# One chunk of a weights' product from split operands, and another sequence of pieces, in a fused attention, gating and spatial-product kernel

## The chip, the cores and the metric

The kernel runs on one core of a Trainium2 chip. The metric is the device time of one launch in microseconds, taken as the median of several runs; one more execution was taken by the hardware profiler, and all rows and durations below come from it.

## The reference, cut to what matters

Three layers run one after the other on a batch of 2 sequences of 768 positions with 512 channels (8 heads of 64). All is float32.

```python
# 1: attention; scores of near keys (within 16) and of the maxima of 32-key blocks
x = softmax(concat(mask(q @ k.T), q @ k_max.T + log 32)) @ concat(v, v_mean)
# 2: causal convolution of 5 taps as a gate
gate = sigmoid(conv5(x, conv_w))
x = (gate * (x @ w_val)) @ w_out
# 3: spatial gating
h = relu(x @ w_in)                 # 512 -> 1024
u, v = h[..., :512], h[..., 512:]
v_s = w_spatial @ normalize(v) + b_spatial
out = (u * v_s) @ w_out2
```

Between layers 2 and 3 nothing stands but two products, so the kernel multiplies the weights first, `w_out @ w_in` (512 x 512 by 512 x 1024), and applies one matrix to the gated values. This **weights' product** is where the change acts.

## The kernel before, in words

**Pieces and threads.** The work is written as some forty threads (generators) that each yield after a piece: `lk`, `lq`, `lv` load one pair of heads of k, q, v; `kw` lays out a pair's keys; `score`, `at` and `pv` are scores with softmax, transposition, and attention times values with the convolution; `gate`, `val0`/`val1`, `u0`/`u1`, `v0`/`v1`, `ws`, `f0`/`f1`, `s0`/`s1`, `out2` and `r` are the later stages for the two batches; `hot` is a warm-up matmul that nobody reads; `vsum` loads and sums the rows of v by blocks (two loads of 512 KB a piece), `put` sets these means into the values.

**What sets the order.** `ORDER` (line 45) is a list of thread names; each token runs the named thread by one piece (lines 1275 to 1295), and a piece that needs others runs those first (`need`, line 1285). Every operation is only recorded then, and the position in that list is its priority. A planner (lines 214 to 420) afterwards simulates the engines with its own costs and gives each engine, at each moment, the operation that can start first, and among several that can start (within `LOOK`, line 43, 100 ns on GpSimd, 200 on SyncE, 0 on the others) the one of the earliest priority. It also hands out the 33 SBUF units and the 8 PSUM banks; banks are given strictly in the order of the recorded list. All loads go through SyncE's queue in the planner's order. All engine calls leave through line 230, so every row of the profile has L230, and tiles come by the names of their homes (`at_u` an SBUF unit, `at_ps` a PSUM bank); rows are told apart by form.

**Weights.** Weights come as raw 64-bit words (`load64`, line 553): 512 KB for 128 rows of 512, turned into float32 by a ScalarE pass into PSUM and two VectorE passes. A weight that is used "split" is stored as two parts, `hi` (a cast to float32r on ScalarE) and `lo` (the rest, a subtraction on GpSimd), and a product of split operands is three float32r matmuls, hi·hi, hi·lo and lo·hi (`mm3`, line 515), in place of one float32 matmul.

**The weights' product** (`w_product`, line 1198, thread `wp`) has two halves: n = 1 for the V half (columns 512 to 1023 of w_in), then n = 0 for the U half. Each half is four output blocks `e` of 128 x 512, and each block sums four chunks `i` of 128 rows, so there are eight chunks of four matmuls. The V half runs over chunks outside and blocks inside, with four PSUM banks open at once (line 1219), one piece a chunk; the U half runs over blocks outside (line 1205, `OUTER` = 1), one piece a block. `WHOLE` (line 38) says for each half how many of its chunks use the float32 operands whole; before, all four of both. The pieces of w_in are loaded by `in1` (V half) and `in0` (U half), those of w_out (transposed) by `wout`; whether a piece is split at load is decided in `split64`:

```python
whole = i < WHOLE[max(c, name == "ot")] and name in ("ot", "in")   # line 574
```

For w_out (`name == "ot"`) this asks the V half's number. Where the U half wants a piece of w_out split that the V half wants whole, the thread `os` (`split_late`, line 1193) splits it later; before, that thread has no pieces (line 1254).

The results are split again into hi and lo (`wv` for V, `wu` for U, line 1179) and used by `v0`, `v1`, `u0`, `u1`.

Of the kernel before, what the change touches and what calls it, by code (L numbers as in the profile page):

```python
# [34 lines left out]
OUTER, PSUMT = 1, 1  # L35


WHOLE = {0: 4, 1: 4}


SEVEN = {'val': (), 'u': (), 'v': ()}
# [1 line left out]
LOOK = {"PE": 0, "ACT": 0, "DVE": 0, "POOL": 100, "SP": 200}  # L43

ORDER = """
    in1 mask*2 hot wout hot*2 wout hot lk kw in1 lk lq wp hot*2 wout kw in1*2 lq hot score*2 wout vsum wp in0 lk in0
    wval lk wp lq in0 lq at vsum lv*2 wp lk kw score put cw lq in0 wp at kw score wu score wval lq score lk lv put*2
    score pv wp score wp at wp wval lv pv lk pv lq at wval at put pv gate val0*2 at lv lk val0 at pv val0 kw at
    score*2 pv vsum*2 wu kw wu*2 wv pv*2 gate u0*4 lq put at val0 at wv lv kw val0 score*3 kw score*3 wv*2 v0*2 val0
    at val0 at pv put pv at lv put v0 at*2 v0 at u0 pv*4 f0 lv put pv gate pv ws v0 u0 v0 u0 val1 ws gate val1 u0  # L50
    val1 s0 val1*3 ws v1 val1 out2 v1 val1 s0 f0 u1*2 f0 v1*2 f1 v1 u1 ws v1 u1 s0 out2 s0 u1 s1 u1 f0 ws f1 f0 s0
    u1 ws f1 u1 s0 s1 out2 s0 out2 ws s0*3 f0*2 s0*2 s1 f1 s1 r s1 r s1 s0 f1 s0 f1 r s1 r*2 f1 s1*2 r s1*3 r s1 r*2
    s1 r*3
"""

WIN = 10240 / 3
# [393 lines left out]
def tile_kernel(ctx, tc, q, k, v, vn, w_val, conv_w, w_out, w_in, w_sp, b_sp, w_out2, mask_l, mask_r, eye, out):  # L450
# [120 lines left out]
    def split64(name, src, c):  # L571
        third = Parts(512)
        for i in range(KT):
            whole = i < WHOLE[max(c, name == "ot")] and name in ("ot", "in")
            t = load64(src[i * P : (i + 1) * P, 1024 * c : 1024 * (c + 1)], to=wide.get() if whole else None)
# [603 lines left out]
    def halves(x):  # L1179
        hi, lo = third.get(), third.get()  # L1180
        copy("phi", hi, x)
        sub("plo", lo, x, f(hi))
        return hi, lo
# [9 lines left out]
    def split_late(i):  # L1193
        need("wout", i + 1)
        if i >= WHOLE[0]:
            W["ot", i, 0] = halves(T["ot", i, 0])

    def w_product():
# [5 lines left out]
        for n in (1, 0):  # L1204
            if n < OUTER:
                for e in range(KT):
                    po = psum()
                    for i in range(KT):
                        need("wout", i + 1)
                        need(f"in{n}", i + 1)  # L1210
                        if i < WHOLE[n]:
                            pe.matmul(po, T["ot", i, 0][:, e * P : (e + 1) * P], T["in", i, n], start=i == 0, stop=i == KT - 1)
# [7 lines left out]
            for i in range(KT):  # L1220
                need("wout", i + 1)
                need(f"in{n}", i + 1)
                if i < WHOLE[n]:
                    for e in range(KT):
# [60 lines left out]
    def need(name, n):  # L1285
        plan.needs.setdefault(plan.piece[-1], set()).add((name, n))
        while count[name] < n:
            step(name)
# [86 lines left out]
```

## Time and profile before

| | us |
|---|---|
| median of 3 runs | 262.67 |
| lowest, highest | 261.48, 264.2 |
| the profiled execution | 262.76 |
| its span, first to last instruction | 261.0 |
| TensorE busy in it | 254.6 |
| VectorE, ScalarE, GpSimd busy | 188.8, 158.9, 161.0 |

In the rows PE is TensorE, PEld its weight loads, DVE VectorE, ACT ScalarE, POOL GpSimd, SP SyncE (SPq: its queue, which issues the loads). Times are microseconds from the span's start unless marked ns. Matmuls are pipelined and their ends are modelled, so a stretch of matmuls is best read from its start to the next row's start. The float32 matmul of this kernel stands as two instructions, one from float32r operands as one; both print as f32.

### The profile page before, as it was taken

How to read it: one execution, taken by the hardware profiler on the slowest of the kernel's cores; microseconds unless marked ns; L12 is line 12 of the kernel's file. 1: busy time of each engine (PE TensorE's matmuls, PEld its weight loads, DVE VectorE, ACT ScalarE, POOL GpSimd, SP SyncE). 2: the span in 40 equal slices, each digit the busy share in tenths (PEclk: the TensorE clock that was granted, in tenths of full speed). 3: DMA queues.
4: the chain of work that ended last, by engine and by line, in shares of the span. 5: the costliest groups of instructions: out<-in, count | busy, mean ns of one | idle time of the engine just before them, and what ended most of it. 6: DMA issues, size and time to landing. Idle time of an engine off the chain costs nothing.

```text
span 261.0 us, 5401 instructions
## 1 busy us (share of the span) xinstructions
PE 254.6 (98%) x1878; PEld 217.7 (83%) x1878; DVE 188.8 (72%) x558; ACT 158.9 (61%) x440; POOL 161.0 (62%) x189
## 2 busy tenths in 40 slices
PE   7899999999999999999999999999999999999995
PEld 5355665588999989899999999899999989889884
DVE  1789979599999995779996785879777915545110
ACT  2578989999897999859352254152385534233122
POOL 6233508998977649933907449346289998885110
PEclk9999999999999999999999999999999999999999
DMA  6999999899140006740000010003022003021213
GB/s 216 400 411 407 404 222 353 268 346 291 45 124 0 4 9 180 236 133 0 4 1 0 0 52 31 0 0 83 1 82 83 0 0 121 3 80 40 80 43 121
DMA packets 10651, 31.80 MB, mean 122 GB/s; under 512 B 1520, under 2 KB 1984, under 8 KB 10624
## 3 DMA queue, kind: packets, MB, share of 16 engines
q1 hardware_dynamic: 10592, 31.43, 35.7%
q8 instruction: 15, 0.25, 0.4%
q14 instruction: 12, 0.10, 0.1%
q0 software_dynamic: 32, 0.02, 0.0%
HBM read 28.20 MB, written 3.15 MB: 120 GB/s over the span
## 4 chain that ended last, share of the span: by engine, by line
PE 75%; DMA 11%; ACT 6%; DVE 5%; issue 2%; POOL 1%; SPq 0%; POOLq 0%; DVEq 0%; ACTq 0%
PE at_ps L230 75%; DMA at_u<-in_k_dram 6%; ACT at_u L230 5%; DMA at_u<-in_vn_dram 4%; DVE at_u L230 4%; POOL at_u L230 1%; SPq L230 0%; ACT at_ps L230 0%; DVE km L230 0%; ACT xl L230 0%; POOLq L230 0%; DVE nm L230 0%; DVEq L230 0%; ACTq L230 0%
## 5 line engine op out<-in xcount | busy, mean ns | idle before, releaser
L230 PE MATMUL at_ps<-at_u,at_u 128*128 128x384 f32 (+4 forms) x1744 | 229.1, 319 | 0.7 <-POOL at_u L230 0.4
L230 PEld LDWEIGHTS at_ps<-at_u,at_u 128*128 128x128 f32 (+2 forms) x1744 | 198.8, 186 | 27.2 <-issue 9.9
L230 POOL TENSOR_TENSOR at_u<-at_u,at_u 128x384 fp32r<-128x384 f32 (+2 forms) x83 | 101.2, 1245 | 44.2 <-ACT at_u L230 43.8
L230 ACT CAST at_u<-at_u 128x384 fp32r<-128x384 f32 (+2 forms) x83 | 45.8, 589 | 44.1 <-DVE at_u L230 31.6
L230 ACT COPY at_u<-at_ps 120x384 f32<-120x384 f32 (+3 forms) x61 | 28.6, 508 | 31.5 <-PE at_ps L230 31.5
L230 DVE TENSOR_TENSOR at_u<-at_ps,at_u 128x384 f32<-128x384 f32 (+1 forms) x36 | 19.8, 552 | 32.5 <-PE at_ps L230 25.7
L230 POOL TENSOR_TENSOR at_u<-at_u,sm 128x360 f32<-128x360 f32 x32 | 25.9, 836 | 20.8 <-DVE sm L230 17.2
L230 ACT ACTIVATE at_u<-at_u,nm 128x120 f32<-128x120 f32 x96 | 36.6, 386 | 1.8 <-DVE nm L230 1.8
L230 DVE SCALAR_TENSOR_TENSOR at_u<-at_ps,cw,at_u 128x384 f32<-128x384 f32 (+3 forms) x64 | 36.5, 605 | 0.2
L230 DVE CUSTOM_DVE_ANT_0 at_u<-at_ps,mask 128x120 f32<-128x120 f32 x96 | 21.8, 273 | 1.0 <-PE at_ps L230 1.0
L230 ACT ACTIVATE at_ps<-at_u 128x512 f32<-128x512 f32 x20 | 13.1, 654 | 9.9 <-DMA at_u<-in_moe_w_out_dram 5.9
L230 ACT ACTIVATION_READ_ACCUMULATOR at_u<-at_u,nm 128x1 f32 x96 | 18.4, 191 | 0.0
L230 POOL COPY at_u<-at_u 128x320 f32<-128x320 f32 (+2 forms) x24 | 17.4, 730 | 1.2
L230 DVE TENSOR_SCALAR at_u<-at_u 128x512 uint32<-128x512 uint32 (+1 forms) x21 | 12.7, 607 | 6.7 <-DMA at_u<-in_moe_w_in_dram 5.3
L230 DVE TENSOR_TENSOR at_u<-at_u,at_u 128x256 f32<-128x256 f32 (+2 forms) x25 | 15.7, 633 | 1.4 <-DMA at_u<-in_vn_dram 1.3
L230 POOL TENSOR_TENSOR va<-va,power 128x1 f32<-128x1 f32 x12 | 7.6, 638 | 14.6 <-DVE va L230 14.6
L230 DVE SCALAR_TENSOR_TENSOR at_u<-at_u,at_u 128x384 f32<-128x384 f32 x16 | 16.2, 1019 | 0.3
L230 ACT ACTIVATE at_u<-at_ps 128x512 f32<-128x512 f32 x20 | 11.6, 598 | 7.2 <-PE at_ps L230 7.2
L230 DVE TENSOR_TENSOR at_u<-at_u 128x384 f32<-128x384 f32 (+5 forms) x31 | 14.8, 477 | 0.1
L230 DVE SCALAR_TENSOR_TENSOR at_u<-at_ps,at_u 128x512 uint32<-128x512 uint32 x20 | 13.6, 686 | 1.4 <-ACT at_ps L230 0.5
L230 PEld LDWEIGHTS at_ps<-moves,at_u 128*120 128x120 f32 x96 | 10.9, 137 | 3.7 <-issue 1.6
L230 PE MATMUL at_ps<-moves,at_u 128*120 128x128 f32 x96 | 13.6, 276 | 0.1
(38 smaller groups left out, 136.5 us busy)
## 6 DMA issues: line engine op xcount, KB each, us to landing
at_u<-in_moe_w_in_dram SPq DMA_DIRECT2D x8, 512.0 KB
at_u<-in_moe_w_out_dram SPq DMA_DIRECT2D x8, 512.0 KB, 9.6
at_u<-in_k_dram SPq DMA_DIRECT2D x8, 384.0 KB, 7.2
at_u<-in_q_dram SPq DMA_DIRECT2D x8, 384.0 KB, 6.2
at_u<-in_vn_dram SPq DMA_DIRECT2D x6, 512.0 KB
at_u<-in_v_dram SPq DMA_DIRECT2D x8, 384.0 KB, 7.3
out_dram<-at_u SPq DMA_DIRECT2D x11, 256.0 KB, 2.0
at_u<-in_moe_w_spatial_dram SPq DMA_DIRECT2D x6, 384.0 KB, 4.1
```

The lines of the kernel that those rows point to most:

```text
L230: getattr(real, method)(*[home(x) for x in args], **{k: home(x) for k, x in kw.items()})
```

## The change

`WHOLE[0]` goes from 4 to 3: the fourth chunk (i = 3) of the U half's four blocks is computed from split operands by `mm3`, in place of float32 ones. With that, w_in's fourth piece of the U half is split at load (`split64`), and the thread `os` gets four pieces, of which the fourth splits w_out's fourth piece (the first three only state their need). `ORDER` is replaced by another sequence, which has the `os` pieces in it. The planner, its costs and every other piece are the same.

```diff
-WHOLE = {0: 4, 1: 4}
+WHOLE = {0: 3, 1: 4}
...
 ORDER = """
-    in1 mask*2 hot wout hot*2 wout hot lk kw in1 lk lq wp hot*2 wout kw in1*2 lq hot score*2 wout vsum wp in0 lk in0
-    wval lk wp lq in0 lq at vsum lv*2 wp lk kw score put cw lq in0 wp at kw score wu score wval lq score lk lv put*2
-    score pv wp score wp at wp wval lv pv lk pv lq at wval at put pv gate val0*2 at lv lk val0 at pv val0 kw at
-    score*2 pv vsum*2 wu kw wu*2 wv pv*2 gate u0*4 lq put at val0 at wv lv kw val0 score*3 kw score*3 wv*2 v0*2 val0
-    at val0 at pv put pv at lv put v0 at*2 v0 at u0 pv*4 f0 lv put pv gate pv ws v0 u0 v0 u0 val1 ws gate val1 u0
-    val1 s0 val1*3 ws v1 val1 out2 v1 val1 s0 f0 u1*2 f0 v1*2 f1 v1 u1 ws v1 u1 s0 out2 s0 u1 s1 u1 f0 ws f1 f0 s0
-    u1 ws f1 u1 s0 s1 out2 s0 out2 ws s0*3 f0*2 s0*2 s1 f1 s1 r s1 r s1 s0 f1 s0 f1 r s1 r*2 f1 s1*2 r s1*3 r s1 r*2
-    s1 r*3
+    mask hot mask wout in1 wout lk in1 kw lk lq in1 wout hot*2 lq kw hot*2 in1 hot wp score*2 wp vsum wp wout in0 lk
+    kw lk in0 lq kw wval at lq in0 vsum os score*2 lv lq lv lk*2 os put cw pv put score wp hot os*2 in0 wp at wval
+    wp score lv score wp at pv lk wu lv put at score pv wp at put pv gate at wval kw wval val0 at val0*2 pv kw pv
+    val0 wu at lv score*2 vsum pv at wu kw pv gate vsum put lv wu u0*3 at lk wv u0 val0*2 lv lq score put wv kw
+    score lv lq score wv score lq score wv score val0*2 v0*2 at pv*2 at v0 at put at v0 at*2 u0 pv*4 put pv*2 u0 ws
+    u0 ws v0 f0 gate u0 gate val1*3 v0 val1 f0 val1*3 u1 s0*2 val1 ws v1 u1 f0 v1 f0 out2 u1 f0 v1 f1 u1 s0 u1 v1*3
+    u1 out2 ws*2 s0 f1 u1 out2 s0*5 s1 out2 u1 s1 s0 f1 r f0 s1 f1 ws r s1*3 ws s0 s1 f1 s0 f0 s0 s1*2 s0 r s1 r*4
+    f1 s1*2 r f1 s1*2 r*4
 """
```

## Rows read from the trace of the kernel before

**Rows 1.** The page: span, and busy time of each engine

```profile
span 261.0 us, 5401 instructions
...
PE 254.6 (98%) x1878; PEld 217.7 (83%) x1878; DVE 188.8 (72%) x558; ACT 158.9 (61%) x440; POOL 161.0 (62%) x189
```

**Rows 2.** The chain of waits, last pieces: start, duration, what

```profile
62.51 195.46 PE at_ps L230 x1411
...
257.99 0.37 ACT at_u L230
```

**Rows 3.** Table of stretches: busy time of each engine

```profile
core 0: us, PE busy (x) PEld busy (x) DVE busy (x) ACT busy (x) POOL busy (x), PEclk, DMA share, GB/s
...
8.00:20.00 12.00, 11.55 (x67) 6.19 (x68) 9.15 (x30) 7.93 (x21) 4.74 (x11) 1.00 1.02 405
20.00:31.00 11.00, 11.00 (x61) 5.80 (x62) 10.66 (x37) 10.32 (x30) 4.41 (x12) 1.00 1.03 404
...
40.00:50.00 10.00, 9.79 (x51) 4.72 (x49) 9.06 (x42) 9.91 (x43) 8.86 (x10) 1.00 0.86 304
50.00:60.00 10.00, 9.72 (x123) 7.63 (x125) 7.90 (x15) 9.96 (x26) 9.63 (x10) 1.00 1.02 342
...
80.00:100.00 20.00, 20.00 (x230) 18.56 (x229) 18.57 (x101) 18.41 (x76) 13.72 (x20) 1.00 0.05 11
```

**Rows 4.** TensorE in order of time, 8 to 28 us

```profile
8.25 3.67 PE L230 MATMUL at_ps<-at_u 128*128 128x512 f32 x8 [0.74 <-DVE at_u L230]
...
12.54 1.08 PE L230 MATMUL at_ps<-at_u,at_u 64*64 64x120 f32 x12 [0.17 <-POOL at_u L230]
...
14.70 1.07 PE L230 MATMUL at_ps<-at_u,at_u 64*64 64x120 f32 x12
...
18.48 1.09 PE L230 MATMUL at_ps<-at_u,at_u 64*64 64x120 f32 x24
19.50 3.70 PE L230 MATMUL at_ps<-at_u 128*128 128x512 f32 x8
23.04 1.88 PE L230 MATMUL at_ps<-at_u,at_u 128*128 128x512 f32 x4
24.75 0.82 PE L230 MATMUL at_ps<-moves,at_u 128*120 128x128 f32 x6
25.41 2.74 PE L230 MATMUL at_ps<-at_u,at_u 128*128 128x512 f32 x6
```

**Rows 5.** TensorE in order of time, around 105 us

```profile
104.61 3.01 PE L230 MATMUL at_ps<-at_u,at_u 128*128 128x512 f32 x12
107.46 1.47 PE L230 MATMUL at_ps<-moves,at_u 128*120 128x128 f32 x12
```

**Rows 6.** Groups of instructions by form: count, busy us, mean ns, idle before

```profile
L230 POOL TENSOR_TENSOR at_u<-at_u,at_u 128x512 fp32r<-128x512 f32 x16 | 21.4, 1347 | 7.3 <-ACT at_u L230 7.0
...
L230 DVE SCALAR_TENSOR_TENSOR at_u<-at_ps,at_u 128x512 uint32<-128x512 uint32 x20 | 13.6, 686 | 1.4 <-ACT at_ps L230 0.5 <-PE at_ps L230 0.2
...
L230 ACT ACTIVATE at_ps<-at_u 128x512 f32<-128x512 f32 x20 | 13.1, 654 | 9.9 <-DMA at_u<-in_moe_w_out_dram 5.9 <-DMA at_u<-in_moe_w_in_dram 4.0
...
L230 ACT CAST at_u<-at_u 128x512 fp32r<-128x512 f32 x16 | 9.6, 625 | 1.1 <-DVE at_u L230 1.1
```

**Rows 7.** SyncE's queue in order of time; the page's loads of w_out

```profile
8.98 0.33 SPq L230 DMA_DIRECT2D at_u<-in_moe_w_out_dram  x1
10.36 1.43 SPq L230 DMA_DIRECT2D at_u<-in_vn_dram  x2
...
36.65 0.33 SPq L230 DMA_DIRECT2D at_u<-in_moe_w_in_dram  x1
...
at_u<-in_moe_w_out_dram SPq DMA_DIRECT2D x8, 512.0 KB, 9.6
```

## The prediction

> **What bounds the kernel now.** I read the page first: TensorE is busy 254.6 of the 261.0 us span; VectorE, the next, 188.8 us [rows 1]. The chain of waits says the same from the other end: its last link but one is an unbroken run of 195.46 us of matmuls that begins at 62.51 us [rows 2]. From there on, nothing but the sum of TensorE's work sets the end, and a changed sequence can gain nothing, only open a gap. So the second view is the table of stretches, to see where TensorE is not full [rows 3]: between 8 and 20 us it idles 0.45 us, between 40 and 50 us 0.21, between 50 and 60 us 0.28, together 0.94 us; 20 to 31 us and 80 to 100 us are full. Before 8.25 us it runs only warm-up matmuls. The granted clock is 1.00 in each of these stretches, so the higher of the two levels (2.4 GHz). The same table shows what feeds it: between 8 and 31 us the loads run at 404 to 405 GB/s with the DMA engines 100% occupied. Up to about 40 us the order of loads decides which pieces TensorE can take; between 40 and 60 us ScalarE (9.91 and 9.96 of 10 us) and GpSimd (8.86 and 9.63) are nearly full as well. The early 60 us are the place where this change acts, in both of its parts.
>
> **The split chunk on TensorE.** The weights' product has eight chunks of four matmuls with 512 columns. A float32 one stands in the trace as two instructions: a chunk is the row of x8 at 19.50 us, which runs until the next row begins at 23.04, so 3.54 us, 0.443 us an instruction [rows 4]. From split operands a chunk takes 4 x 3 = 12 matmuls, each one instruction. The nearest row is a product of twelve such instructions with 512 columns at 104.61 us, with the next row at 107.46: 2.85 us, 0.238 each [rows 5]. The chunk costs 3.54 - 2.85 = 0.69 us less. Lower bound of the gain nothing (if TensorE stands waiting for data there in any case), upper bound 0.69; I take -0.69 us, because the row is the same form and size, and because all that TensorE saves early counts in full once the run from 62.51 us starts sooner.
>
> **The splits that it needs.** Two operands are split that were used whole: w_in's fourth piece of the U half, and w_out's fourth piece. Each is one cast on ScalarE and one subtraction on GpSimd, 128x512: 2 x 625 ns and 2 x 1347 ns [rows 6], in all 1.25 us and 2.69 us. VectorE gets nothing. w_out's split has time (the piece lands long before the U half needs it). w_in's is on the way: its load is issued at 36.65 us in the profile of before [rows 7], it lands into the stretch where both engines are nearly full, and only then can the last chunk of the four U products close. Its cover is other TensorE work (scores, transposes, attention times values), which fills 9.79 of 10 us there [rows 3]. If that cover were gone, TensorE would wait for one cast and one subtraction, 0.63 + 1.35 = 1.97 us; a gain from this term is excluded, as it only adds work. Nearer to the rows is the covered case (two gaps of 0.21 and 0.28 us in the whole stretch): I take +0.1 us.
>
> **The new sequence: loads.** Expanding both sequences by their needs gives SyncE's order. The first ten loads are the same kinds in nearly the same order (w_out before w_in instead of after at the very start, which lands both at the same moment; third w_in and w_out pieces exchanged; the second q before the fourth w_in). The one move with a price is w_out's fourth piece: before, it is the twelfth load, issued at 8.98 us ahead of the two loads of the value rows at 10.36 us [rows 7]; now it comes behind them. These two are 2 x 512 KB; at 405 GB/s it lands 1.05 MB / 405 GB/s = 2.6 us later. It is half of the last chunk of the V half. Before, it landed about 8.98 + 9.6 = 18.6 us (the page's time to landing [rows 7]), and conversion from 64 bit takes at least a ScalarE pass and a VectorE pass, 654 + 686 ns [rows 6], so it could be used from about 20.0 us; TensorE came to that chunk at 23.04 us without a gap [rows 4]. At best the 3.0 us of slack hide the 2.6 us entirely. At worst the slack was used up by the queue on VectorE up to the moment of use, and the chunk begins 2.6 us late; in that case TensorE has two transposition pieces in hand (0.82 us for the one at 24.75 us) and the seventh warm-up matmul, so 2.6 - 2 x 0.82 = 1.0 us is idle. (With the second transposition not ready, 1.8.) Below nothing: nothing of this move brings work forward by more than the 0.45 us idle of this stretch. Range -0.45 to +1.8, I take +0.3 us.
>
> **The new sequence: pieces on TensorE.** Before, the first scores piece falls into halves around a matmul: x12 in 1.08 us at 12.54 and x12 in 1.07 us at 14.70, while a whole one of x24 at 18.48 takes 1.09 us [rows 4]. Half a piece costs as much as a whole one, so a piece cut in two costs 1.06 us more. The changed sequence has the first scores pieces behind the first chunk again, but the loads around them differ; it may mend this cut (-1.06) or make a second one (+1.06). Slightly likelier mended than doubled, as there is one to mend and none is seen in the other rows: -0.3 us. Behind 62.51 us the sequence also differs in many places (values, U, V, spatial product, results); before is full there, so this is worth nothing or costs a gap. The last pieces of the spatial product are followed by results that were ready before, in both sequences, so the tail keeps its cover. I take 0; bound +1.0, one chain of the kind that a cast and a subtraction make without cover.
>
> **Sum.** -0.69 + 0.1 + 0.3 - 0.3 + 0 = -0.59 us. The profiled execution took 262.76 us (261.0 span and 1.76 around it); 262.76 - 0.59 = 262.17, so 262.2 us. The median of the runs shown is 262.67, 0.09 below the profiled one, a difference that I leave out.
>
> **The rivals.** (1) Slower: the V half's accumulators stay open. Its four products are gathered side by side over all four chunks, so four of eight PSUM banks are held from 8.25 us until the last chunk, which before ended at about 27.1 us (four instructions at 23.04, four of the six at 25.41 [rows 4]). Scores take two banks a piece, each load one, each transposition one. If w_out's fourth piece closes the half 2.6 us late, the U half has to start behind it, and its own last chunk then meets the 1.97 us of the new split on full engines. For: the loads are the limit up to 31 us, and rows 3 show no spare time in 20 to 31 us. Against: the transpositions and scores that can run between. Price: 2.6 + 1.97 - 2 x 0.82 - 0.69 = +2.24 us, and scores pieces that get their two banks late are cut, one more of them +1.06: +3.3 us, thus 266.1 us; it decides when the last chunk of the V half ends behind 29.7 us (27.1 + 2.6). (2) Faster: the early losses are mended. All of the 0.94 us idle and the cut piece go, beside the chunk: -0.69 - 0.94 - 1.06 = -2.69 us, 260.1 us. For: each of these is a fault of sequence alone, and the sequence is new. Against: 0.45 us of it lies under loads at 405 GB/s, which no sequence makes faster. (3) The change does not do what it says: TensorE stands waiting at the chunk's place, the 0.69 us become idle time, and the other terms stay as summed: 262.76 + 0.1 = 262.9 us. For: the U half's last chunk waits for a load and a split in every case. Against: TensorE has no gap over 0.3 us a stretch there, so it always had another piece.
>
> (4) A gap early makes the clock fall. The granted clock was 1.00 in all of 8 to 100 us [rows 3], with scores and loads between the products, so nothing of before bears this out; if a chunk of 3.54 us ran at the lower level, it would take 7.08, and the time would be 262.2 + 3.5 = 265.7 us. The Trainium skill, page "TensorE: Matmul & The Clock Gate", section "HAM oscillation — how this bites in real kernels", has this as a rule: bursts of matmuls that wait for loads in between start again at the lower clock. In this trace the loads' stretch ran without such a fall, so the rule gets a small chance.
>
> **How the numbers follow.** Forecast (between 261.0 and 263.5 us) 0.60; (3) and small mishaps up to 265.3, 0.15; (1) 0.10, (4) 0.03; (2) 0.12. A change of 1%, about 2.6 us, is what a measurement of this kernel can tell from none: faster means below 260.0, slower above 265.3 us. All of (1) and (4) count as slower, together 0.13; (2) lies on the border, and I count 0.11 of it as faster, the rest as the same: 0.76. The range: its lower end is (2) with a little of repeat scatter (the three runs spread from 261.48 to 264.2), 259.8; its upper end takes the bounds of the loads (+1.8) and of the split (+1.97) with the chunk's gain gone in part, 262.76 + 1.8 + 1.97 - 0.69 = 265.8, of which I leave the last 0.8: 265.0 us. Outside lies about 0.2.
>
> **What the changed profile would show.** Right: the weights' product is 56 float32 instructions (two a matmul) and 12 from split operands; TensorE's busy time about 0.7 us less; the run of matmuls that ends the chain starts within 1 us of 62.5; no stretch behind 64 us with over 0.3 us idle. The term of the loads is seen at the first chunk's end and at a gap between 23 and 27 us; the term of the split as waits of TensorE's weight loads on GpSimd between 38 and 50 us; the cut as rows of scores with x12. Wrong: a gap of over 1 us behind 64 us, where I see nothing to lose; a granted clock below 1.00 between 8 and 250 us; or a saving that stems from the stretch behind 64 us.

## The result, and the profile after

The changed kernel takes 263.93 us (median of 20 runs, 263.54 to 264.45) where the kernel before takes 262.33 (20 runs, 261.25 to 264.2): ratio 1.0055, 95% interval 1.004 to 1.007. It is slower by 1.4 us by the ratio (1.6 by the medians) where 0.6 us less was forecast. The profiled execution of the changed kernel is its slowest run, 264.45 us, with a span of 262.7; it lies 0.5 us above its median and that of before 0.4 above its own, so the two profiles can be compared. One run further down, of the version with four moves, took 416.92 us at a granted clock of 0.562 in the mean, and its ratio leaves it out.

The page of the kernel after answers to [rows 1]:

```profile
span 262.7 us, 5391 instructions
...
PE 253.9 (97%) x1882; PEld 219.7 (84%) x1882; DVE 189.3 (72%) x558; ACT 160.6 (61%) x442; POOL 163.6 (62%) x191
```

TensorE works 0.7 us less and the span is 1.7 us longer, so TensorE must stand idle more. The last pieces of the chain of waits, against [rows 2], say how far on:

```profile
63.42 0.69 DVE at_u L230
64.15 195.53 PE at_ps L230 x1399
```

The unbroken run of matmuls is as long as before (195.53 against 195.46 us) and begins 1.64 us later. All of the loss lies ahead of 64 us, and the piece in front of that run is VectorE's. The table of stretches tells where; first the three stretches of the kernel before that stand not in [rows 3], then the kernel after (columns as there):

```profile
0.00:8.00 8.00, 5.64 (x12) 3.87 (x12) 2.14 (x4) 2.60 (x3) 4.14 (x20) 1.00 0.74 253
...
31.00:40.00 9.00, 9.00 (x128) 6.19 (x124) 7.33 (x51) 7.73 (x40) 2.21 (x4) 1.00 1.03 270
...
60.00:80.00 20.00, 19.91 (x226) 18.51 (x223) 19.60 (x58) 19.07 (x57) 16.53 (x22) 1.00 0.43 126
```

```profile
0.00:8.00 8.00, 5.52 (x13) 4.07 (x14) 2.62 (x5) 2.89 (x4) 4.22 (x20) 1.00 0.78 256
8.00:20.00 12.00, 10.88 (x65) 5.61 (x65) 8.89 (x38) 8.58 (x28) 4.77 (x11) 1.00 1.02 404
20.00:31.00 11.00, 10.45 (x92) 6.21 (x92) 10.69 (x25) 8.48 (x20) 5.70 (x12) 1.00 1.04 408
31.00:40.00 9.00, 8.64 (x70) 4.97 (x67) 8.20 (x49) 8.57 (x40) 2.09 (x2) 1.00 1.01 263
40.00:50.00 10.00, 10.00 (x80) 6.24 (x77) 9.20 (x44) 9.46 (x40) 9.29 (x12) 1.00 0.86 292
50.00:60.00 10.00, 9.53 (x103) 7.82 (x98) 9.02 (x18) 10.00 (x28) 7.99 (x10) 1.00 1.00 307
60.00:80.00 20.00, 19.27 (x245) 18.22 (x245) 19.90 (x56) 18.43 (x55) 16.65 (x23) 1.00 0.60 184
80.00:100.00 20.00, 20.00 (x231) 19.04 (x230) 19.02 (x104) 18.78 (x71) 13.50 (x18) 1.00 0.10 31
```

Length less TensorE's busy time is its idle time. Between 8 and 80 us that was 0.45 + 0 + 0 + 0.21 + 0.28 + 0.09 = 1.03 us; now it is 1.12 + 0.55 + 0.36 + 0 + 0.47 + 0.73 = 3.23, so 2.20 more. Ahead of 8 us it is 0.12 more. 2.20 + 0.12 - 0.7 (less work) = 1.62 us, which is the 1.64 us by which the run begins later. The granted clock is 1.00 in every stretch of both, the higher of its two levels. The account is closed: the saving came, and 2.2 us of new idle time ate it. TensorE in order of time has them one by one:

```profile
12.61 1.08 PE L230 MATMUL at_ps<-at_u,at_u 64*64 64x120 f32 x12 [1.11 <-POOL at_u L230]
...
14.76 1.08 PE L230 MATMUL at_ps<-at_u,at_u 64*64 64x120 f32 x12
...
30.26 1.07 PE L230 MATMUL at_ps<-at_u,at_u 64*64 64x120 f32 x20 [0.55 <-DVE at_u L230]
31.27 0.71 PE L230 MATMUL at_ps<-moves 128*128 128x264 f32 x2
...
34.38 1.12 PE L230 MATMUL at_ps<-at_u 128*128 128x512 f32 x2 [0.36 <-DVE at_u L230]
...
53.28 2.12 PE L230 MATMUL at_ps<-at_u,at_u 128*128 128x512 f32 x8 [0.47 <-POOL at_u L230]
...
64.15 2.03 PE L230 MATMUL at_ps<-at_u,at_u 128*128 128x384 f32 x10 [0.73 <-DVE at_u L230]
```

Read the releasers. The first gap is mostly a change of label: the first scores start at 12.61 us as they did at 12.54 before [rows 4], only the seventh warm-up matmul, which stood in front of them, now stands at 31.27. Of the other four, three end with a VectorE operation, and the fourth (53.28) with GpSimd's subtraction of w_in's fourth piece, the very operand of the split chunk. So the next view is VectorE and GpSimd in order of time at those places, VectorE's rows first, then GpSimd's:

```profile
28.03 1.38 DVE L230 TENSOR_SCALAR at_u<-at_u 128x512 uint32<-128x512 uint32 x1
29.51 0.69 DVE L230 SCALAR_TENSOR_TENSOR at_u<-at_ps,at_u 128x512 uint32<-128x512 uint32 x1
...
47.51 1.19 DVE L230 TENSOR_SCALAR at_u<-at_u 128x512 uint32<-128x512 uint32 x1
...
61.50 1.49 DVE L230 TENSOR_SCALAR at_u<-at_u 128x512 uint32<-128x512 uint32 x1
```

```profile
27.83 1.28 POOL L230 TENSOR_TENSOR at_u<-at_u,at_u 128x512 fp32r<-128x512 f32 x1
...
46.95 3.07 POOL L230 COPY at_u<-at_u 24x1536 f32<-24x1536 f32 x2
...
61.41 1.28 POOL L230 TENSOR_TENSOR at_u<-at_u,at_u 128x512 fp32r<-128x512 f32 x1
```

The `TENSOR_SCALAR` of 128x512 is the first VectorE pass of a weight (a shift of raw words). Undisturbed it takes 0.43 us, as a row further down shows. Here it takes 1.38, 1.19 and 1.49 us, each time beside a GpSimd operation that began 0.1 to 0.6 us before it; such a coincidence is called a meeting below. The first of these GpSimd operations (27.83) is the subtraction that the split of w_out's fourth piece adds. The shifts at 28.03 and 47.51 belong to the second and the fourth piece of w_in for the U half, the one at 61.50 to the fourth piece of w_val, whose second pass (63.42 to 64.11) reads the PSUM bank that TensorE writes next; that is what it waits for at 64.15. This gave the theory to be tested: VectorE's shifts meet GpSimd's long operations, and TensorE pays.

### The profile page after: what moved, and what is told of

Same layout as the page of the kernel before. It is cut to its first block, busy times and chain, and to the rows that moved or that the text cites. A ratio compares the mean times of both kernels' runs of the same rounds, so it can differ in the third digit from the quotient of the medians.

```text
span 262.7 us, 5391 instructions
## 1 busy us (share of the span) xinstructions
PE 253.9 (97%) x1882; PEld 219.7 (84%) x1882; DVE 189.3 (72%) x558; ACT 160.6 (61%) x442; POOL 163.6 (62%) x191
## 4 chain that ended last, share of the span: by engine, by line
PE 79%; DVE 7%; DMA 5%; ACT 4%; issue 2%; POOL 1%; SPq 0%; DVEq 0%; POOLq 0%
PE at_ps L230 79%; DVE at_u L230 7%; ACT at_u L230 4%; DMA at_u<-in_vn_dram 3%; DMA at_u<-in_k_dram 2%; POOL at_u L230 1%; DVE km L230 1%; SPq L230 0%; DVE nm L230 0%; DVE sm L230 0%; DVEq L230 0%; ACT xl L230 0%; POOLq L230 0%
## 5 line engine op out<-in xcount | busy, mean ns | idle before, releaser
L230 PE MATMUL at_ps<-at_u,at_u 128*128 128x384 f32 (+4 forms) x1740 | 225.6, 317 | 2.9 <-POOL at_u L230 1.6
L230 PEld LDWEIGHTS at_ps<-at_u,at_u 128*128 128x128 f32 (+2 forms) x1740 | 199.0, 186 | 26.3 <-issue 7.3
L230 POOL TENSOR_TENSOR at_u<-at_u,at_u 128x384 fp32r<-128x384 f32 (+2 forms) x85 | 104.8, 1257 | 46.9 <-ACT at_u L230 45.3
L230 ACT CAST at_u<-at_u 128x384 fp32r<-128x384 f32 (+2 forms) x85 | 47.2, 593 | 43.7 <-DVE at_u L230 32.9
L230 ACT COPY at_u<-at_ps 120x384 f32<-120x384 f32 (+3 forms) x61 | 28.6, 513 | 26.0 <-PE at_ps L230 25.8
L230 DVE TENSOR_TENSOR at_u<-at_ps,at_u 128x384 f32<-128x384 f32 (+1 forms) x36 | 19.8, 554 | 30.3 <-PE at_ps L230 27.8
L230 ACT ACTIVATE at_u<-at_u,nm 128x120 f32<-128x120 f32 x96 | 36.6, 385 | 1.7 <-DVE nm L230 1.7
L230 DVE SCALAR_TENSOR_TENSOR at_u<-at_ps,cw,at_u 128x384 f32<-128x384 f32 (+3 forms) x64 | 36.2, 606 | 0.1
L230 POOL TENSOR_TENSOR at_u<-at_u,sm 128x360 f32<-128x360 f32 x32 | 24.8, 803 | 16.4 <-DVE sm L230 7.0
L230 DVE CUSTOM_DVE_ANT_0 at_u<-at_ps,mask 128x120 f32<-128x120 f32 x96 | 21.4, 274 | 1.7 <-PE at_ps L230 1.4
L230 ACT ACTIVATE at_ps<-at_u 128x512 f32<-128x512 f32 x20 | 13.2, 659 | 12.8 <-DMA at_u<-in_moe_w_out_dram 7.9
L230 POOL COPY at_u<-at_u 128x320 f32<-128x320 f32 (+2 forms) x24 | 18.0, 756 | 2.1 <-DMA at_u<-at_u 0.9
L230 ACT ACTIVATION_READ_ACCUMULATOR at_u<-at_u,nm 128x1 f32 x96 | 18.2, 190 | 0.0
L230 DVE TENSOR_TENSOR at_u<-at_u,at_u 128x256 f32<-128x256 f32 (+2 forms) x25 | 17.6, 702 | 0.7 <-DMA at_u<-in_vn_dram 0.6
L230 ACT ACTIVATE at_u<-at_ps 128x512 f32<-128x512 f32 x20 | 11.3, 608 | 9.5 <-PE at_ps L230 9.5
L230 DVE TENSOR_SCALAR at_u<-at_u 128x512 uint32<-128x512 uint32 (+1 forms) x21 | 13.0, 621 | 5.0 <-DMA at_u<-in_moe_w_out_dram 4.0
L230 PE MATMUL at_ps<-at_u 128*128 128x512 f32 x32 | 15.5, 607 | 1.0 <-DVE at_u L230 1.0
L230 DVE TENSOR_TENSOR at_u<-at_u 128x384 f32<-128x384 f32 (+5 forms) x31 | 15.8, 515 | 0.2
L230 POOL TENSOR_TENSOR va<-va,power 128x1 f32<-128x1 f32 x12 | 7.1, 599 | 13.4 <-DVE va L230 13.4
L230 DVE SCALAR_TENSOR_TENSOR at_u<-at_ps,at_u 128x512 uint32<-128x512 uint32 x20 | 13.8, 689 | 1.7 <-ACT at_ps L230 0.4
L230 DVE SCALAR_TENSOR_TENSOR at_u<-at_u,at_u 128x384 f32<-128x384 f32 x16 | 14.4, 920 | 0.1
L230 DVE BATCH_NORM_STATS2 st<-at_u 128x6 f32<-128x512 f32 x12 | 8.1, 686 | 8.9 <-ACT at_u L230 8.9
```

The lines of the kernel that those rows point to most:

```text
L230: getattr(real, method)(*[home(x) for x in args], **{k: home(x) for k, x in kw.items()})
```

## The experiments

In most runs below the planner was not asked to choose: it was given the recorded order of every engine and the recorded homes of the tiles, so that only the named operations move. The calls then leave through another line, and rows print L316 for L230. Ratios are to the kernel before on the same chip, with the 95% interval.

**The two parts of the change by themselves.** First the new sequence with no split: the order of after is replayed, the chunk is float32 again, and the two casts and two subtractions are gone.

```diff
-WHOLE = {0: 3, 1: 4}
+WHOLE = {0: 4, 1: 4}
```

> The changed kernel with its sequence on every engine replayed instruction by instruction, but the fourth chunk of the U half in float32 again: the two casts and two subtractions are gone, each block's three last matmuls are one. Theory A (the added subtractions and casts stand in the way of VectorE and ScalarE, and that costs more than the chunk saves): TensorE's 0.69 us come back, but the gaps behind them at 30.26 us (0.55) and 53.28 us (0.47) go, so 263.93 + 0.69 - 1.02 = 263.6 us, ratio to the kernel before about 1.005. Rival B (the sequence alone is the whole cost and the split is worth its 0.69 us): 264.6 us, ratio 1.009. Rival C (the split is the whole cost): 262.3 us, ratio 1.000.

Measured: 265.56 us (6 runs), ratio 1.0122 (1.0091 to 1.0153), span 263.9, slower than all three theories had it. The gaps at 30.26 and 53.28 us are gone, but others of 2.39 us in all stand between 13 and 66 us, mostly behind ScalarE (first two rows). VectorE's rows below show which meetings need the split: the shift of w_in's second piece is down to 0.42 us, the one of w_val's fourth still takes 1.50.

```profile
56.00 1.04 PE L316 MATMUL at_ps<-moves,at_u 128*120 128x128 f32 x6 [0.80 <-ACT at_u L316]
...
62.56 2.45 PE L316 MATMUL at_ps<-at_u,at_u 128*128 128x384 f32 x53 [0.43 <-ACT at_u L316]
```

```profile
27.99 0.42 DVE L316 TENSOR_SCALAR at_u<-at_u 128x512 uint32<-128x512 uint32 x1
...
62.73 1.50 DVE L316 TENSOR_SCALAR at_u<-at_u 128x512 uint32<-128x512 uint32 x1
```

Then the split with the old sequence (the planner chooses the order anew here, so more than the split differs):

```diff
-WHOLE = {0: 4, 1: 4}
+WHOLE = {0: 3, 1: 4}
```

> The kernel before with its own sequence, and only the number changed that has the U half's fourth chunk computed from split operands; planned anew. If the split is worth its 0.69 us in any sequence: 261.6 us, ratio 0.997. If it needs a sequence with room for it (two more operands in SBUF, four PSUM banks held until the subtraction is through, GpSimd's 2.69 us in a full stretch): 264 us or more, ratio over 1.006.

Measured: 268.18 us (6 runs), ratio 1.0206 (1.0176 to 1.0235). Gaps stand all over it, behind 80 us too, where every other kernel here is full:

```profile
80.00:100.00 20.00, 19.22 (x220) 17.70 (x219) 19.89 (x101) 18.56 (x65) 12.56 (x19) 1.00 0.01 3
```

What follows: the two parts do not add up. The sequence alone costs about 3.2 us, the split in a new plan of the old sequence about 5.4, both together 1.4. Within its sequence the split is thus worth some 1.8 us by the ratios, 1.1 more than the chunk's 0.69; why ScalarE's gaps come when it is taken out is open. A sequence belongs to the split that it was drawn up with. That the loss sits in the early part of the sequence was tried directly, in the kernel before, with the old tokens up to the first U piece and the rest in the new order behind them, all in float32 and planned anew:

```diff
 ORDER = """
...
-    score*2 pv vsum*2 wu kw wu*2 wv pv*2 gate u0*4 lq put at val0 at wv lv kw val0 score*3 kw score*3 wv*2 v0*2 val0
...
+    score*2 pv vsum*2 wu kw wu*2 wv pv*2 gate at kw put lv u0*3 at u0 val0*2 lv score put wv kw score lv score wv
...
```

> The kernel before (all chunks float32) with a sequence made of two: the tokens of the old one up to the first piece of the U product, then what is left in the order of the new one, planned anew. Theory A (all of the loss lies ahead of about 64 us, and the new sequence behind it costs nothing): the time of the kernel before, 262.3 to 262.8 us, ratio 0.998 to 1.003. Rival (part of the loss stems from the new order of the later stages): 263.3 us or more.

Measured: 265.52 us (6 runs), ratio 1.0128 (1.0086 to 1.017). Up to 80 us its table of stretches is that of before, and behind 100 us TensorE is full; but a gap of 1.3 us stands at the seam of the two sequences, around 91 us. So the rival's time came, 263.3 us or more, but the gap at the seam has a part in it; behind 100 us the late part of the new sequence opens no gap of its own, and the time of this run says nothing more.

**The loads.** w_out's fourth load goes back ahead of the two loads of the value rows, as it stood before:

```diff
 SyncE's queue
-load of value rows x2, load of w_out (4th piece)
+load of w_out (4th piece), load of value rows x2
```

> The changed kernel replayed, with one load moved on SyncE: w_out's fourth piece goes ahead of the two loads of value rows, where the kernel before has it. My prediction's term of the loads, if it is the cause: the V half's last chunk no longer comes late, time down by 0.5 to 1 us, 263.2 us. Theory A: the chunk already ran without a gap behind the third (23.75 us, after a transposition that was due anyway), so the time stays within 0.2 us of 263.9 us.

Measured: 264.61 us (6 runs), ratio 1.0084 (1.0057 to 1.0111): no gain, and 0.7 us more than theory A had. In the kernel after that load is issued at 11.51 us (first row), 2.5 us later than before [rows 7], and TensorE has no gap from 12.61 to 29.7 us. Put back (second row), it gives TensorE a gap where there was none (third row):

```profile
11.51 0.33 SPq L230 DMA_DIRECT2D at_u<-in_moe_w_out_dram  x1
```

```profile
8.62 0.33 SPq L316 DMA_DIRECT2D at_u<-in_moe_w_out_dram  x1
...
24.41 5.89 PE L316 MATMUL at_ps<-at_u,at_u 128*128 128x512 f32 x60 [0.60 <-DVE at_u L316]
```

**The subtraction that the split adds, moved away.** GpSimd's subtraction of w_out's fourth piece, which lies beside the shift at 28.03 us, goes behind the one of w_val's first piece:

```diff
 GpSimd's queue
-..., subtraction (w_out, 4th piece), subtraction (w_val, 1st piece)
+..., subtraction (w_val, 1st piece), subtraction (w_out, 4th piece)
```

> The changed kernel replayed, with one instruction moved on GpSimd: the subtraction that splits w_out's fourth piece goes from its place at 27.83 us to behind the one of w_val's first piece, into the stretch where GpSimd is idle (34.6 to 39.3 us). Theory A: VectorE's shift at 28.03 us takes 0.4 in place of 1.38 us, the gap of 0.55 us at 30.26 goes, the time falls by 0.3 to 0.6 us, to about 263.4 us (ratio 1.004). Rival (TensorE is bound elsewhere in this stretch, by loads): the shift gets shorter and the time stays at 263.9 us.

Measured: 266.06 us (6 runs), ratio 1.0142 (1.0107 to 1.0177): slower than the kernel after. Yet the shift did what the theory says. VectorE, GpSimd and TensorE in order of time, and the stretch from 31 us:

```profile
27.98 0.43 DVE L316 TENSOR_SCALAR at_u<-at_u 128x512 uint32<-128x512 uint32 x1
...
32.37 2.49 POOL L316 TENSOR_TENSOR at_u<-at_u,at_u 128x512 fp32r<-128x512 f32 x2 [4.54 <-ACT at_u L316]
34.90 0.69 DVE L316 SCALAR_TENSOR_TENSOR at_u<-at_ps,at_u 128x512 uint32<-128x512 uint32 x1 [2.19 <-POOL at_u L316]
35.65 1.54 PE L316 MATMUL at_ps<-at_u 128*128 128x512 f32 x2 [2.25 <-DVE at_u L316]
```

```profile
31.00:40.00 9.00, 6.75 (x18) 3.31 (x17) 6.65 (x35) 7.30 (x34) 2.70 (x3) 0.81 1.03 255
```

The same shift at the same moment takes 0.43 us with GpSimd idle, 1.38 with the subtraction beside it, and the gap at 30.26 is gone. But the later subtraction holds its source tile, which VectorE's next weight pass is to overwrite: VectorE waits 2.19 us, TensorE 2.25, and in that stretch the granted clock is 0.81 in the mean, so part of it ran at the lower level. The six runs show the two losses apart: three took 265.31 to 265.36 us at a mean clock of 0.998 to 1.000, three 266.76 to 267.01 at 0.992 to 0.993, the profiled one (266.89) among them. Without a fall of the clock the kernel is thus 1.1 us slower than the kernel after by the ratios, and the fall adds some 1.5. A subtraction on GpSimd thus costs in two ways: by what it runs beside, and by the tile that it keeps.

**The meeting taken apart from VectorE's side.** Instead of the subtraction, the shift of w_in's second piece moves ahead of the operation before it, so that it starts ahead of the subtraction:

```diff
 VectorE's queue
-shift (in0, 1st piece), second pass (in0, 1st), shift (in0, 2nd piece)
+shift (in0, 1st piece), shift (in0, 2nd piece), second pass (in0, 1st)
```

> The changed kernel replayed, with one instruction moved on VectorE: the shift of w_in's second piece of the U half (28.03 us, 1.38 us long, in which GpSimd runs the added subtraction of w_out's fourth piece) goes ahead of the operation before it, so that it is through before that subtraction begins. Theory A (GpSimd's subtraction holds up VectorE's shift, and TensorE waits for it): the shift takes 0.4 to 0.7 us, the gap of 0.55 us at 30.26 goes. If that reaches the end: 263.4 us; if TensorE waits for VectorE again at 64.15: 263.9 us, with that gap larger. Rival (the shift is long for another reason): it stays at 1.4 us in its new place.

Measured: 263.51 us (12 runs), ratio 1.0038 (1.0017 to 1.0059). VectorE, GpSimd and TensorE in order of time:

```profile
26.41 0.77 DVE L316 TENSOR_SCALAR at_u<-at_u 128x512 uint32<-128x512 uint32 x2
27.09 1.27 DVE L316 SCALAR_TENSOR_TENSOR at_u<-at_ps,at_u 128x512 uint32<-128x512 uint32 x2
...
26.18 0.71 POOL L316 MEMSET at_u<- 128x32 f32 x1
...
62.33 2.53 PE L316 MATMUL at_ps<-at_u,at_u 128*128 128x384 f32 x13 [0.71 <-DVE at_u L316]
```

The four passes now fill 26.41 to 28.36 us; in the kernel after they took from 26.60 to 30.20. The gaps at 30.26 and 34.38 are gone. The median is 0.4 us lower, but this ratio's interval meets that of the kernel after (1.004 to 1.007). The gap ahead of the long run (62.33) stays, 0.71 us, so the next move is there: GpSimd's subtraction of w_val's third piece goes behind the three short operations that followed it.

```diff
 GpSimd's queue
-subtraction (w_val, 3rd piece), copy (5th key tile), zeroing (6th), copy (5th)
+copy (5th key tile), zeroing (6th), copy (5th), subtraction (w_val, 3rd piece)
```

> The changed kernel replayed, with one instruction moved on GpSimd: the subtraction of w_val's third piece (61.41 to 62.69 us) goes behind three short copies of the key windows, so that VectorE's shift of w_val's fourth piece (61.50 us, 1.49 us long) meets short instructions. Theory A: the last bound of the early stretch is VectorE at 64.15 us, which waits behind this shift; the shift takes at most 0.9 us, the gap of 0.73 us shrinks by 0.4 to 0.7 us, and this one reaches the end, since behind 64 us TensorE has no gap: 263.4 us (ratio 1.003). Rival (the PSUM bank or operand that TensorE waits for there comes from elsewhere): time within 0.2 us of 263.9 us.

Measured: 263.55 us (12 runs), ratio 1.004 (1.002 to 1.0059). The shift takes 0.67 us in place of 1.49, and TensorE is full from 60 to 80 us (19.27 before the move); the interval again meets that of the kernel after:

```profile
59.49 2.01 POOL L316 COPY at_u<-at_u 24x1536 f32<-24x1536 f32 x2
...
61.13 0.67 DVE L316 TENSOR_SCALAR at_u<-at_u 128x512 uint32<-128x512 uint32 x1
```

```profile
60.00:80.00 20.00, 20.00 (x247) 18.82 (x242) 19.33 (x58) 18.61 (x57) 16.98 (x24) 1.00 0.62 189
```

Both moves together:

```diff
+both moves above
```

> The changed kernel replayed with both moves that gained: w_in's shift ahead of the added subtraction (on VectorE) and w_val's subtraction behind the short copies (on GpSimd). Theory A (each move takes away one stall of VectorE under a GpSimd subtraction, and one gap of TensorE): the gains add, 263.93 - 0.42 - 0.38 = 263.1 us, or 262.8 if the gap of 0.71 us that the first move left at 62.3 us goes in full; ratio to the kernel before 1.001 to 1.003. Rival (both moves win time that the same later wait swallows): 263.5 us, as with one alone.

Measured: 263.11 us (12 runs), ratio 1.0015 (0.9995 to 1.0034). This interval lies below that of the kernel after: together the two moves give some 0.8 to 1.0 us (by the medians, by the ratios). That each gives 0.4 and the two add is what the medians say; no single move is clear of the noise.

**Two things that gave nothing by themselves.** GpSimd's zeroing of the fifth key tile stands 1.72 us at the head of its queue (50.02 to 51.74 us in the kernel after), with the split's own subtraction behind it. It was moved to about 62 us:

```diff
 GpSimd's queue
-zeroing (5th key tile), subtraction (w_in, 4th U piece)
+subtraction (w_in, 4th U piece), ..., zeroing (5th key tile)
```

> The changed kernel replayed, with one instruction moved on GpSimd: the small memset of the fifth pair's key windows, which waits at the head of its queue from 50.02 to 51.74 us with the subtraction of w_in's fourth piece behind it, goes behind to the copies it belongs to at 62.6 us. If the wait of the new split is what TensorE's gap of 0.47 us at 53.28 stems from: the subtraction starts at about 50.2, the gap goes, and the GpSimd work behind it comes up to 1.5 us earlier; time down by 0.4 to 1.0 us, 263.2 us. Rival (the gap is only moved on, since at about 64 us TensorE waits for VectorE whatever comes before): the time stays within 0.2 us of 263.9 us, and the gap at 64.15 grows by what the other lost.

Measured: 264.04 us (8 runs), ratio 1.0066 (1.0042 to 1.009). The gap at 53.28 is gone, but one of 0.35 us behind GpSimd has come at 56.26, and the one ahead of the long run stays with 0.74 us. Then the seventh warm-up matmul, 0.55 us of TensorE:

```diff
-warm-up matmul, the seventh
```

> The changed kernel replayed without its seventh warm-up matmul, which runs at 31.27 us between useful pieces (the kernel before ran it at 11.76 us in a stretch in which TensorE waited for the key windows anyway). If TensorE is the bound at that point: 0.55 us less, 263.4 us. Rival (behind it TensorE waits for VectorE, 0.36 us at 34.38 and 0.73 us at 64.15 in any case): nothing, 263.9 us, and these gaps grow by 0.55 us.

Measured: 264.09 us (9 runs), ratio 1.0057 (1.0036 to 1.0078). Work taken from TensorE gives nothing either: the gap ahead of the long run, now at 63.86 us, is still 0.72, and from 31 to 40 us TensorE is busy 8.24 us in place of 8.64. So 0.40 of the 0.55 us are waited away at once, behind VectorE, in gaps of 0.23 us at 31.75 and 0.53 at 34.56. Both were tried again with the two moves, first together, then the zeroing alone:

```diff
+the two moves, the zeroing moved, no seventh warm-up
```

> As the run with two moves, and with the two that won nothing alone: the small memset goes out of the way of w_in's subtraction, and the seventh warm-up matmul is gone. Theory A (they won nothing alone because TensorE waited for VectorE at 64 us in any case; with that wait gone they count): 0.4 and 0.55 us less than with two moves, 262.1 us, level with the kernel before or below it (ratio 0.996 to 1.001). Rival (they are worth nothing): the time of the run with two moves, 262.8 to 263.1 us.

Measured: 262.99 us (12 runs), ratio 1.0012 (0.999 to 1.0033); expected was 262.1.

```diff
+the two moves, the zeroing moved
```

> The order of the kernel after with three moves: the shift of w_in's second U piece ahead of the operation before it, GpSimd's subtraction of w_val's third piece behind three short copies, and GpSimd's zeroing of the fifth key tile at 62.6 us; the seventh warm-up stays where it is. Theory (GpSimd's long operations and their place are what the sequence loses): with VectorE's late end at 64 us gone, the wait at 52 us now counts, and its removal, which alone gave nothing, gives 0.3 to 0.4 us: 262.7 us, ratio about 1.000, no TensorE gap over 0.3 us between 13 and 80 us. Rival (the warm-up left out is what held the run of four moves at 263.0): this one stands below 262.8 with every run's granted clock at 0.998 or more. Rival (the wait at 52 us is made good elsewhere anyway): 263.1 us, as with the two moves.

Measured: 263.36 us (12 runs), ratio 1.0031 (1.0008 to 1.0053); expected was 262.7. Against the two moves alone neither is faster beyond the intervals: the theory in the form "only these two meetings" had missed something.

**The third meeting.** It was in the rows above (47.51) and in the run of two moves stood out more, the shift of w_in's fourth U piece, which the split chunk waits for:

```profile
46.34 1.62 DVE L316 TENSOR_SCALAR at_u<-at_u 128x512 uint32<-128x512 uint32 x1
```

It was moved ahead of three operations of a scores piece, first with the zeroing left in its place:

```diff
 VectorE's queue
-scores x3, shift (in0, 4th piece)
+shift (in0, 4th piece), scores x3
```

> The order of the kernel after with the two moves that gained (the shift of w_in's second U piece, the subtraction of w_val's third piece) and one more of the same kind: on VectorE the shift of w_in's fourth U piece stands ahead of three operations of a scores piece, so that it starts before GpSimd's copy of the value means (in the run of two moves it ran from 46.34 to 47.96 us beside that copy). GpSimd's zeroing of the fifth key tile stays where it is, ahead of the subtraction of that piece. Theory (a VectorE shift that meets a long GpSimd operation is what costs): the shift takes 0.4 to 0.5 us again, ScalarE's cast no longer stands 0.98 us at the head of its queue, the TensorE gap of 0.27 us at 49.46 goes and the one at 52.55 shrinks or goes: 262.6 us, ratio 0.999. Rival (the rest is ScalarE, which is full from 50 to 60 us in every version): the shift is short, but the time stays at 263.1 us. Rival (the zeroing, which waits at the head of GpSimd's queue): the same 263.1 here, and only the run beside it is faster.

Measured: 262.78 us (12 runs), ratio 1.0008 (0.9986 to 1.0031). The gaps around 49 and 52 us are gone; one of 0.32 us behind ScalarE is at 45.24, and one of 0.62 us behind a load of q at 27.84. With the zeroing moved as well:

```diff
 GpSimd's queue
-copy x2, zeroing (5th key tile), subtraction (w_in, 4th U piece)
+copy x2, subtraction (w_in, 4th U piece), ..., zeroing (5th key tile)
```

> As the run beside it, and GpSimd's zeroing of the fifth key tile also moved to about 62 us, so that the subtraction of w_in's fourth U piece follows GpSimd's two copies at once. Theory (the meetings of VectorE and GpSimd cost, and what stands behind them comes free one after the other): shift short, cast early, subtraction from about 49.3 instead of 51.2 us, no TensorE gap over 0.3 us between 13 and 80 us: 262.3 us, ratio 0.998. Rival (ScalarE full from 50 to 60 us): 263.1 to 263.4 us, as with two and three moves, with a TensorE gap that follows a ScalarE operation in that stretch.

Measured: 262.5 us (12 runs), ratio 0.9987 (0.997 to 1.0004). From 13 us on no gap of TensorE is over 0.27 us. VectorE and GpSimd in order of time, and the start of the long run:

```profile
45.44 0.66 DVE L316 TENSOR_SCALAR at_u<-at_u 128x512 uint32<-128x512 uint32 x1
...
46.26 3.08 POOL L316 COPY at_u<-at_u 24x1536 f32<-24x1536 f32 x2 [0.45 <-DMA at_u<-at_u]
```

```profile
59.45 198.19 PE at_ps L316 x1452
```

Four moves, of which three take meetings apart, bring the kernel from ratio 1.0055 to 0.9987, 1.8 us, with the same matmuls on the same split operands. The run of three moves differs from this one in the third shift alone, and its interval (1.0008 to 1.0053) does not meet this one (0.997 to 1.0004): that one move is worth 0.9 us by the medians and 1.2 by the ratios, the clearest of all. With the zeroing left in its place the same move shows nothing beyond the noise (263.11 to 262.78), and what the zeroing's move gives with the shift gone (262.78 to 262.5) lies within the intervals of the two runs. Whether 262.5 us is faster than the kernel before is not shown, as the interval holds 1. Last, with the meetings apart, the seventh warm-up again:

```diff
+the four moves, no seventh warm-up
```

> The order with the four moves (the shift of w_in's second U piece, the shift of its fourth, the subtraction of w_val's third piece, the zeroing of the fifth key tile), and the seventh warm-up matmul left out, which took 0.55 us of TensorE at about 30 us and whose result nobody reads. Theory (with VectorE no longer late, TensorE's own work sets the time from 13 us on): 0.4 to 0.55 us less than with the four moves, 262.0 us, ratio 0.996. Rival (something else sets the pace behind it, ScalarE from 40 to 60 us first of all): 262.5 us as with the four moves, with a gap of TensorE behind a ScalarE or GpSimd operation between 31 and 60 us that is longer by the same half microsecond.

Measured: 262.69 us (12 runs), ratio 0.9994 (0.9976 to 1.0011): no gain, the rival stands. The stretch from 40 us and one of TensorE's gaps:

```profile
40.00:50.00 10.00, 9.49 (x72) 5.78 (x71) 8.80 (x41) 10.00 (x45) 9.21 (x12) 1.00 0.82 272
```

```profile
45.41 2.99 PE L316 MATMUL at_ps<-at_u,at_u 64*64 64x120 f32 x16 [0.51 <-ACT at_u L316]
```

ScalarE is busy 10.00 of 10 us from 40 to 50 us, and TensorE now waits for it, and 0.64 us for a load of q at 28.03 us. That load's wait stands in the profiles of three of the last versions (0.31, 0.62 and 0.64 us) and not in two others of nearly the same order, so it goes with when a load happens to land; it may be a reason why runs of one version differ by a microsecond, which is not shown. A second one is on record for the slowest runs: 264.89 us (the two moves, the zeroing moved, no seventh warm-up) and 264.66 us (the two moves and the third shift) both had a mean granted clock of 0.987, where the other 22 runs of these versions had 0.998 to 1.000.

## Why the prediction was wrong

The step that failed: the sum had no term for VectorE ending late ahead of 62.51 us. The splits were priced by their work on ScalarE and GpSimd alone, with "VectorE gets nothing" and +0.1 us, and of the gaps that a new sequence may open only those behind 62.51 us were asked for. The runs showed something else: 2.2 us of new idle time of TensorE ahead of 64 us. Three of its four real gaps end with a VectorE operation, and four moves, three of which take VectorE's shifts away from GpSimd's operations, give back 1.8 us.

- **The chunk, -0.69 us: right.** TensorE's busy time fell by 0.7 us. Alone that would not settle it, as runs with the same matmuls at full clock spread from 252.9 to 254.0 us; but in the run of two moves the chunk's twelve matmuls take 1.03 + 1.95 = 2.98 us, where 3.54 were to go and 2.85 to come.
- **The splits, +0.1 us: wrong.** VectorE got no instruction, but it lost time: the subtraction of w_out's fourth piece made a VectorE shift 0.95 us longer (1.38 against 0.43). The path of w_in's fourth piece, which the split alone makes urgent, met a GpSimd copy at its shift (1.19 us; 1.62 in the run of two moves). The kernel's text had the price: its planner marks such VectorE operations (`lock`, line 197) and holds them back behind GpSimd's in its simulation (line 301).
- **The sequence's pieces, -0.3 us: wrong.** The cut scores piece is neither mended nor doubled (x12 at 12.61 and at 14.76 us as in [rows 4]), so that term is 0; and gaps ahead of 62 us had no price. The meeting at 61.50 us is of pieces that both kernels have, and it stands in the run without the split too (1.50 us at 62.73): the new sequence brought them together. "Behind 62.51 us ... I take 0" was right: TensorE is full there.
- **The sequence's loads, +0.3 us: refuted.** The load came 2.5 us later, as worked out, and cost nothing; its slack of 3.0 us held. Moved back, it made the kernel no faster.
- **The signs.** The long run was to start within 1 us of 62.5 and started at 64.15; the busy time and the stretch behind 64 us came as said.
- **The rivals.** That the gain is hidden came nearest in mechanism, though not by the wait that it named. The V half closed without a gap (TensorE unbroken from 12.61 to 29.7 us), and the clock stayed at 1.00. The one on the slower side that happened was not on the list: two engines that slow each other without a wait between them.
- **The sum.** Forecast -0.6, measured +1.4 us by the ratio. The difference is the 2.2 us of new idle time. That the time still lies inside the stated range is the width of the range, which was drawn for the loads and the split's wait. The prediction took 1% as the least difference that can be told; 20 runs of each kernel told 0.55%, give or take 0.15.

Would a view of before have shown the price? Rows 6 do not list the shift. Its group has a mean well above 0.43 us, but nearly the same one in both kernels (before, then after):

```profile
L230 DVE TENSOR_SCALAR at_u<-at_u 128x512 uint32<-128x512 uint32 x20 | 12.5, 629 | 6.7 <-DMA at_u<-in_moe_w_in_dram 5.3 <-POOL at_u L230 0.9 <-DMA at_u<-in_moe_w_out_dram 0.4
...
L230 DVE TENSOR_SCALAR at_u<-at_u 128x512 uint32<-128x512 uint32 x20 | 12.9, 645 | 5.0 <-DMA at_u<-in_moe_w_out_dram 4.0 <-DMA at_u<-in_moe_w_in_dram 0.9
```

So the mean shows that shifts meet something, not that it costs. The kernel before has its longest ones where TensorE is full anyway (these two, and 1.26 us at 199.90), and ahead of 62 us none over 0.96 us:

```profile
157.72 2.00 DVE L230 TENSOR_SCALAR at_u<-at_u 128x512 uint32<-128x512 uint32 x1 [0.42 <-DMA at_u<-in_moe_w_out_dram]
...
196.76 1.43 DVE L230 TENSOR_SCALAR at_u<-at_u 128x512 uint32<-128x512 uint32 x1
```

The kernel after has three of 1.19 to 1.49 us ahead of 64 us and none over 0.80 behind. What changed is where the meetings fall.

Open is what of the last half microsecond is ScalarE's, why the sequence without the split loses more behind ScalarE, and whether a version of this change can be brought clearly below the kernel before.

## What to carry to other kernels

Work added to an engine with idle time is not free when an operation of another engine grows longer beside it, here from 0.43 to 1.38 us: look which of VectorE's operations between two on-chip buffers would run beside the added GpSimd operation, and whether a deadline hangs on them. Rows of one form that differ in length are the sign in a profile; then ask where the long ones stand, because the mean of the group was nearly the same in both kernels (629 and 645 ns) and what had changed was the place. And a gap that goes is not yet time won: the zeroing's move and the missing warm-up matmul each changed the gaps, and neither made the kernel faster beyond the noise, alone or with the last wait gone. Count idle time over the whole early stretch, and believe a move when its interval is clear of the one it is compared with.

## What the runs showed of the hardware

A VectorE shift beside a GpSimd operation that began first ends a fixed time behind it. The GpSimd rows end at 27.83 + 1.28 = 29.11, 61.41 + 1.28 = 62.69, and in the run with w_val's subtraction moved 59.49 + 2.01 = 61.50 us; the shifts beside them end at 29.41, 62.99 and 61.80, 0.30 us later each time. One row speaks for the other way round: in the run with the shift moved first, GpSimd's zeroing at 26.18, 0.12 us long at the same place in the order of the kernel after, took 0.71 us beside VectorE's shifts; GpSimd's row lengths are rough. VectorE operations that read the scores or the passes from PSUM kept their 0.28 and 0.69 us under such subtractions: in the kernel after the pass at 33.64 takes 0.69 us under the subtraction from 33.29 to 34.64. The Trainium skill has the rule, on the page "SBUF — State Buffer", section "Who interferes with whom": VectorE and GpSimd share one pair of ports, and of a VectorE operation in a mode that uses both pairs and a GpSimd operation, the one that issues first holds the shared pair for its whole instruction while the other is blocked; a VectorE operation with at most one SBUF input outside these modes does not contend. The rows above agree with it, the other way round by one row only, and it speaks against the sentence that VectorE gets nothing.

The clock: in the profile of the run with the added subtraction moved, TensorE stood still for 2.25 us, the stretch from 31 to 40 us has a granted clock of 0.81, between its two levels, and the next one 1.00 again. Four float32 instructions behind the gap took from 37.63 to 40.34, 2.71 us, where four at 31.82 in the kernel after took 1.71. Gaps of 1.3 us (around 91 us, in the run of the two sequences) and 1.46 us (ahead of 7.84, with the two moves and the third shift) left the clock at 1.00 in their stretches.
